# Feed-forward products of blocks 1 to 5 by seven half-size products instead of eight, with the attention chunks between them

## The chip, the cores and the metric

The kernel runs on one core of a Trainium2 chip. The metric is the device time of one execution in microseconds (us); of the kernel before, three executions took 854.86, 856.84 and 858.18 us, and their median, 856.84 us, is its time. The engines are named as the profile names them: PE (TensorE, matmuls) with PEld (its weight loads), DVE (VectorE), ACT (ScalarE), POOL (GpSimd) and SP (SyncE, which issues loads). Each engine works through its own instructions in a fixed order and waits for the others on semaphores.

## What is computed

A retention layer (attention with a decaying state) over 4 batches, 8 heads, 768 tokens and 64 channels a head, whose output, as 3072 tokens by 512 channels, goes through a feed-forward layer with a hidden width of 2048. q, k and v are float32; the two weight matrices come as float64.

```python
gamma = 1.0 - 2.0 ** (-5.0 - np.arange(H))
for t in range(S):
    state = gamma[None, :, None, None] * state + np.einsum('bhd,bhe->bhde', k[:, :, t], v[:, :, t])
    y[:, :, t] = scale * np.einsum('bhd,bhde->bhe', q[:, :, t], state)
x = np.ascontiguousarray(y.transpose(0, 2, 1, 3)).reshape(B * S, H * D)
h = x @ w_in                                   # 3072 x 512 by 512 x 2048
g = h * (1.0 / (1.0 + np.exp(-1.702 * h)))
return (g @ w_out).astype(np.float32)          # 3072 x 2048 by 2048 x 512
```

## The kernel before

The tokens are cut into 24 chunks of 128 (six in each batch), and four chunks make a block of 512 tokens, so there are six blocks, 0 to 5. A chunk goes through three stages. `turn` transposes q and k on PE (tile pt, L162) and brings them from PSUM to SBUF as qT and kT, and POOL makes kd, the k decayed to the chunk's end. `attend` multiplies kT and qT on PE (tile pa, L178), and DVE multiplies the result with a mask of decays (at, L181). `finish` adds the state's part and the chunk's own part on PE (tile py: the state's products at L191, those with at and v at L193), brings py into xT, and updates the state (products pu at L205, POOL and DVE behind them).

For a block, `up` makes the hidden units in 16 tiles of 128: four matmuls of 128x128 weights by 512 tokens into ph (L222), the sigmoid on ACT (sg, L224), the product on DVE (gT, L226). `down` makes the output of 128 tokens in 16 matmuls of 512 columns into po (L234), in four parts; a copy (o, L237) and a DMA follow. Each float32 matmul appears as two records in the profile. The main loop puts the stages of the chunks of block m between the units of block m-1, and a scheduler lays the final order on every engine. The loads of q, k and v of a chunk are three DMAs of 256 KB on SP.

The float64 weights are converted on chip (`narrow`, 32 pieces of 128x512): a piece is fetched into a raw buffer (L107), and six DVE steps (L119, L120, L123, L124, L127, L128), two ACT steps (L122, L125) and a POOL multiply (L126) make it float32. Pieces 0 to 15 are w_in's, 16 to 31 w_out's. The conversion runs along the chunks of block 0 and its feed-forward.

Of the kernel before, what the change touches and what calls it, by code (L numbers as in the profile page):

```python
# [9 lines left out]
F32 = mybir.dt.float32  # L10
# [3 lines left out]
P = 128  # L14
# [14 lines left out]
def kernel(  # L29
# [30 lines left out]
    BT = CB * P  # L60
    NB = NCH // CB
    NFF = DFF // P
    WAHEAD = 3
    assert 2 * D == P and HP * P == DM and S % P == 0 and NCH % CB == 0 and DM <= 512

    const = ctx.enter_context(tc.tile_pool(name="const", bufs=1))
    loads = ctx.enter_context(tc.tile_pool(name="loads", bufs=3))
    raw = ctx.enter_context(tc.tile_pool(name="raw", bufs=WAHEAD + 1))
    work = ctx.enter_context(tc.tile_pool(name="work", bufs=2))
    ps_a = ctx.enter_context(tc.tile_pool(name="ps_a", bufs=1, space=bass.MemoryType.PSUM))  # L70
    ps = ctx.enter_context(tc.tile_pool(name="ps", bufs=3, space=bass.MemoryType.PSUM))

# [1 line left out]
    QKV = {}  # L74

    def load(j):
        b, c = divmod(j, NC)
        for name, src in (("q", q), ("k", k), ("v", v)):
            t = loads.tile([P, H, D], F32, name=name + "_in")
            sp.dma_start(t, src[b, :, c * P:(c + 1) * P, :].rearrange("h p d -> p h d"))  # L80
            QKV[name, j] = t

    AHEAD = 2
    rowd = const.tile([P, HP, P], F32, name="rowd")
    cold = const.tile([P, 2 * H + HP], F32, name="cold")
    act.dma_start(cold, col_decay)
    for s in range(2):
        act.dma_start(
            rowd[s * D:(s + 1) * D],
            bass.AP(tensor=row_decay.tensor, offset=row_decay.offset + s * P,  # L90
                    ap=[[0, D], [2 * P, HP], [1, P]]),
        )

    # Weights by pieces of DM columns: w_in's by quarters of its columns, then w_out's by rows.
    W1 = const.tile([P, HP, DFF], F32, name="W1")
    W2 = const.tile([P, NFF, DM], F32, name="W2")
    w1v = moe_w_in.bitcast(U32).rearrange("(c p) (f two) -> p c f two", p=P, two=2)
    w2v = moe_w_out.bitcast(U32).rearrange("(f p) (e two) -> p f e two", p=P, two=2)
    PIECES = [(W1[:, c, f:f + DM], w1v[:, c, f:f + DM]) for f in range(0, DFF, DM) for c in range(HP)]
    N1 = len(PIECES)  # L100
    PIECES += [(W2[:, f, :], w2v[:, f]) for f in range(NFF)]
    RAW = {}

    def fetch(i):
        if i < len(PIECES):
            RAW[i] = raw.tile([P, DM, 2], U32, name="raw")
            sp.dma_start(RAW[i], PIECES[i][1])  # L107

    def narrow(i):
        """float64 to float32: the high word's 20 bits of fraction with the exponent rebiased, plus  # L110
        the low word at its place, added and so rounded in float32, then the sign."""
        fetch(i + WAHEAD)
        w, x = PIECES[i][0], RAW.pop(i)
        lo, hi = x[:, :, 0], x[:, :, 1]
        m = work.tile([P, DM], F32, name="m")
        e = work.tile([P, DM], F32, name="e")
        r = work.tile([P, DM], F32, name="r")
        mu = m.bitcast(U32)
# [4 lines left out]
        dve.tensor_scalar(mu, mu, 4, 1, op0=ALU.logical_shift_left, op1=ALU.logical_shift_right)  # L123
        dve.tensor_scalar(e.bitcast(U32), mu, 0x7F800000, None, op0=ALU.bitwise_and)  # L124
        act.activation(r, lo, AF.Copy, scale=2.0 ** -52)  # L125
        pool.tensor_mul(r, r, e)  # L126
        dve.tensor_add(m, m, r)  # L127
        dve.scalar_tensor_tensor(w.bitcast(U32), hi, 0x80000000, mu, op0=ALU.bitwise_and, op1=ALU.bitwise_or)  # L128

    load(0)  # L130
    for i in range(WAHEAD):
        fetch(i)
        if i < AHEAD - 1:
            load(i + 1)

# [1 line left out]
    ident = const.tile([P, P], F32, name="ident")  # L137
    make_identity(nc, ident)
    # mask[s, i, hp, t] = g^-(s+1) where s <= t, else 0, for head 2 hp + i
    mask = const.tile([P, 2, HP, P], F32, name="mask")  # L140
    for i in range(2):
        for hp in range(HP):
            h = 2 * hp + i
            dve.tensor_copy(mask[:, i, hp, :], cold[:, h:h + 1].to_broadcast([P, P]))
    m3 = mask.rearrange("s i h t -> s (i h) t")
    pool.affine_select(out=m3, in_=m3, compare_op=ALU.is_ge, fill=0.0, base=0,
                       pattern=[[0, H], [1, P]], channel_multiplier=-1)
    # two states in turn, block diagonal over a pair's heads
    state = [const.tile([P, HP, P], F32, name=f"state{i}") for i in range(2)]
    for t in state:  # L150
        dve.memset(t, 0.0)

# [1 line left out]
    QT, KT, KD, AT, XT = {}, {}, {}, {}, {}  # L154

    def turn(j):
        """q and k with channels on partitions, q decayed from the chunk's start; k decayed to its end."""
        qn, kn = QKV.pop(("q", j)), QKV.pop(("k", j))
        for x, store in ((qn, QT), (kn, KT)):
            p = ps.tile([P, HP, P], F32, name="pt", tag="att")  # L160
            for hp in range(HP):
                pe.transpose(p[:, hp, :], x[:, 2 * hp:2 * hp + 2, :].rearrange("p i d -> p (i d)"), ident)  # L162
            t = work.tile([P, HP, P], F32, name="qT" if store is QT else "kT")
# [154 lines left out]
```

## Time and profile before

| what | value |
|---|---|
| median of three runs | 856.84 us |
| lowest and highest run | 854.86 and 858.18 us |
| span of the profiled execution | 855.1 us |
| mean granted clock of TensorE in it | 0.976 |
| HBM read and written | 35.92 MB and 6.29 MB |

The profile shows one execution, from its first to its last instruction; the page gives its span, and no time of that execution beside it, so the span stands against the runs' median. In the page's list of engines each has its busy time, its share of the span and its count of records. The slices cut the span into 40 equal parts; a digit is the busy share in tenths. A group of instructions is given by line, engine, operation, output and inputs; behind the bar stand the busy time in us, the mean length of one in ns, and the idle time before them with what ended it. Lines of the timeline begin with the start and the length in us. Matmuls overlap one another, so the distance from start to start is what one costs in a stream.

### The profile page before, as it was taken

How to read it: one execution, taken by the hardware profiler on the slowest of the kernel's cores; microseconds unless marked ns; L12 is line 12 of the kernel's file. 1: busy time of each engine (PE TensorE's matmuls, PEld its weight loads, DVE VectorE, ACT ScalarE, POOL GpSimd, SP SyncE). 2: the span in 40 equal slices, each digit the busy share in tenths (PEclk: the TensorE clock that was granted, in tenths of full speed). 3: DMA queues.
4: the chain of work that ended last, by engine and by line, in shares of the span. 5: the costliest groups of instructions: out<-in, count | busy, mean ns of one | idle time of the engine just before them, and what ended most of it. 6: DMA issues, size and time to landing. Idle time of an engine off the chain costs nothing.

```text
span 855.1 us, 7038 instructions
## 1 busy us (share of the span) xinstructions
PE 821.2 (96%) x2816; PEld 408.3 (48%) x2816; DVE 239.1 (28%) x434; ACT 126.4 (15%) x210; POOL 84.6 (10%) x91
## 2 busy tenths in 40 slices
PE   4679979999999999999999999999999999999998
PEld 3545434445545544544545454445445445444443
DVE  4877888311222110222111222111122111012000
ACT  2234444000111000111000111100011100011000
POOL 3433333201101000101011000011010000000000
PEclk9759989999999999999999999999999999999999
DMA  9476454012010210110110110111100000000000
GB/s 224 133 183 162 149 164 144 25 38 61 13 25 13 50 38 25 50 25 13 38 49 25 37 36 14 25 46 41 38 13 0 1 12 25 12 1 0 13 13 25
DMA packets 83663, 42.66 MB, mean 50 GB/s; under 512 B 75952, under 2 KB 76464, under 8 KB 83632
## 3 DMA queue, kind: packets, MB, share of 16 engines
q1 hardware_dynamic: 79488, 35.66, 16.5%
q10 hardware_dynamic: 4144, 6.57, 2.1%
q8 instruction: 22, 0.36, 0.2%
q14 instruction: 9, 0.07, 0.0%
HBM read 35.92 MB, written 6.29 MB: 49 GB/s over the span
## 4 chain that ended last, share of the span: by engine, by line
PE 87%; DVE 7%; POOL 3%; issue 2%; DMA 1%; ACT 0%; SPq 0%; POOLq 0%; ACTq 0%; DVEq 0%
PE po L234 39%; PE ph L222 34%; PE py L193 4%; PE py L191 3%; PE pa L178 3%; POOL r L126 2%; PE pu L205 2%; PE pt L162 2%; DVE m L127 2%; DVE e L124 1%; DVE m L123 1%; DMA raw<-in_moe_w_in_dram 1%; DVE W L128 1%; DVE m L119 1%; DVE m L120 1%
## 5 line engine op out<-in xcount | busy, mean ns | idle before, releaser
L222 PE MATMUL ph<-xT,W 128*128 128x512 f32 x768 | 340.8, 601 | 0.0
L234 PE MATMUL po<-W,gT 128*128 128x512 f32 x768 | 336.0, 594 | 0.0
L222 PEld LDWEIGHTS ph<-xT,W 128*128 128x128 f32 x768 | 145.5, 193 | 174.0 <-issue 170.9
L234 PEld LDWEIGHTS po<-W,gT 128*128 128x128 f32 x768 | 143.5, 190 | 170.9 <-issue 169.7
L226 DVE TENSOR_TENSOR gT<-ph,sg 128x512 f32<-128x512 f32 x96 | 66.2, 690 | 209.5 <-ACT sg L224 209.5
L224 ACT ACTIVATE sg<-ph 128x512 f32<-128x512 f32 x96 | 57.2, 595 | 261.8 <-PE ph L222 261.7
L237 DVE COPY o<-po 128x512 f32<-128x512 f32 x24 | 16.6, 692 | 239.2 <-PE po L234 239.2
L171 POOL TENSOR_TENSOR kd<-k_in,cold 128x512 f32<-128x512 f32 x20 | 21.1, 1054 | 451.8 <-PE pu L205 258.1
L193 PE MATMUL py<-at,v_in 128*64 128x128 f32 x384 | 46.8, 321 | 14.4 <-DVE at L181 14.4
L181 DVE TENSOR_TENSOR at<-pa,mask 128x512 f32<-128x512 f32 x48 | 31.2, 683 | 67.1 <-PE pa L178 67.1
L126 POOL TENSOR_TENSOR r<-r,e 128x512 f32<-128x512 f32 x32 | 42.3, 1322 | 72.6 <-DVE e L124 72.4
L198 ACT ACTIVATE xT<-py 128x512 f32<-128x512 f32 x24 | 14.3, 596 | 189.3 <-PE py L193 189.3
L191 PE MATMUL py<-qT,state 128*128 128x128 f32 x160 | 41.3, 344 | 0.0
L178 PE MATMUL pa<-qT,kT 64*128 64x128 f32 x384 | 30.4, 302 | 8.6 <-DVE qT L165 7.8
L191 PEld LDWEIGHTS py<-qT,state 128*128 128x128 f32 x160 | 28.0, 209 | 20.5 <-issue 19.7
L178 PEld LDWEIGHTS pa<-qT,kT 64*128 64x128 f32 x384 | 25.6, 203 | 24.9 <-issue 14.6
L193 PEld LDWEIGHTS py<-at,v_in 128*64 128x64 f32 x384 | 22.5, 148 | 29.6 <-DVE at L181 17.4
L167 ACT ACTIVATE kT<-pt 128x512 f32<-128x512 f32 x24 | 14.3, 596 | 142.4 <-PE pt L162 142.4
L127 DVE TENSOR_TENSOR m<-m,r 128x512 f32<-128x512 f32 x32 | 26.2, 819 | 19.4 <-POOL r L126 19.4
L125 ACT ACTIVATE r<-raw 128x512 f32<-128x512 uint32 x32 | 21.8, 681 | 53.9 <-DVE m L127 43.8
L205 PE MATMUL pu<-v_in,kd 128*128 128x128 f32 x160 | 25.8, 307 | 0.0
L212 POOL TENSOR_TENSOR state<-state,cold 64x256 f32<-64x256 f32 x32 | 20.1, 629 | 49.9 <-DVE state L214 31.8
(25 smaller groups left out, 218.0 us busy)
## 6 DMA issues: line engine op xcount, KB each, us to landing
raw<-in_moe_w_in_dram SPq DMA_DIRECT2D x16, 512.0 KB, 4.5
raw<-in_moe_w_out_dram SPq DMA_DIRECT2D x16, 512.0 KB, 3.3
q_in<-in_q_dram SPq DMA_DIRECT2D x24, 256.0 KB, 4.0
k_in<-in_k_dram SPq DMA_DIRECT2D x24, 256.0 KB, 4.4
v_in<-in_v_dram SPq DMA_DIRECT2D x24, 256.0 KB, 3.3
out_dram<-o ACTq DMA_DIRECT2D x24, 256.0 KB, 2.0
rowd<-in_row_decay_dram ACTq DMA_DIRECT2D x2, 128.0 KB, 5.5
cold<-in_col_decay_dram ACTq DMA_DIRECT2D x1, 10.0 KB, 2.8
```

Of the source, the lines that this page charges most:

```text
L125: act.activation(r, lo, AF.Copy, scale=2.0 ** -52)
L126: pool.tensor_mul(r, r, e)
L127: dve.tensor_add(m, m, r)
L178: pe.matmul(p[:, i, hp, :], KT[j][r, hp, :], QT[j][r, hp, :], start=True, stop=True)
L181: dve.tensor_mul(AT[j][:, i], p[:, i], mask[:, i])
L191: pe.matmul(y[:, hp, :], old[:, hp, :], qt[:, hp, :], start=True, stop=False)
L193: pe.matmul(y[i * D:(i + 1) * D, hp, :], vn[:, 2 * hp + i, :], a[:, i, hp, :], start=not c, stop=True)
L205: pe.matmul(u[:, hp, :], kd[:, h, :].rearrange("p i d -> p (i d)"), vn[:, h, :].rearrange("p i d -> p (i d)"), start=True, stop=True)
L222: pe.matmul(p, W1[:, c, f * P:(f + 1) * P], XT[m][:, c, :], start=(c == 0), stop=(c == HP - 1))
L224: act.activation(s, p, AF.Sigmoid, scale=1.702)
L226: dve.tensor_mul(g, p, s)
L234: pe.matmul(p, GT[m, f][:, n * P:(n + 1) * P], W2[:, f, :], start=(f == 0), stop=(f == NFF - 1))
```

## The change

Block 0 keeps plain products (`up0`, `down0`). For blocks 1 to 5 each of the two feed-forward products is cut in two along tokens, along the summed dimension and along the outputs, and the 2x2 product of parts is made by seven products of parts instead of eight, in Winograd's form of Strassen's method. Slots 0 to 3 of W1, W2, X and G hold the four parts, slots 4 to 6 sums of them (slot 3 is overwritten by a sum as well). `sums_w1` and `sums_w2` make those of the weights once, `sums_x` those of a block's x, all on POOL; `sums_g` changes the hidden units in place on DVE and POOL. The products have 256 columns instead of 512. In `up` four pairs of tiles each go through seven products of four matmuls; ACT copies the accumulator x out between them (p1, u, vv), PE then goes on adding in it, and DVE adds the other accumulators (px and py in the rows; py is also the name of a chunk's output). In `down` the seven products run as 28 units, and a stage of a chunk of the next block follows every second unit.

PE's order is now the order of the code (`manual_schedule`); the scheduler still sets the others. Chunks from 8 on are transposed by DVE in blocks of 32x32, from q and k loaded in 32 DMAs of 16 KB a chunk (q_sq, k_sq), with k loaded once more as it is where kd needs it. For other chunks the transposes stay on PE, and ACT evicts both. The decay of q moves from qT to the eviction of py into X. Within py the four state products come first, then the eight others. In the conversion DVE has four steps, ACT two and POOL two (a clamp, L172, and the multiply, L177); pieces hold other columns, are staged in the slots of W2 that the sums fill later, and have three raw buffers and two sets of temporaries.

```diff
+    ctx.enter_context(tc.manual_schedule(engines={mybir.EngineType.PE}))
...
+        if j < 2 * CB:
+            plain("q", q, "q_sq", 2)
+            plain("kn", k, "k_sq", 2)
+        else:
+            for name, src in (("q", q), ("k", k)):
+                t = two.tile([P, HP, P // C4, C4], F32, name=name + "_sq")
+                for r0 in range(0, P, C4):
+                    d0 = r0 % D
+                    for hp in range(HP):
+                        sp.dma_start(t[r0:r0 + C4, hp],
+                                     src[b, 2 * hp + r0 // D, rows, d0:d0 + C4].rearrange("(s p) d -> p s d", p=C4))
...
-        dve.tensor_scalar(mu, hi, 0x7FFFFFFF, None, op0=ALU.bitwise_and)
-        dve.tensor_scalar(m, m, F64_MOST, F64_LEAST, op0=ALU.min, op1=ALU.max)
-        act.activation(m, m, AF.Copy, scale=2.0 ** 16)
-        dve.tensor_scalar(mu, mu, 4, 1, op0=ALU.logical_shift_left, op1=ALU.logical_shift_right)
-        dve.tensor_scalar(e.bitcast(U32), mu, 0x7F800000, None, op0=ALU.bitwise_and)
+            act.activation(m, hi.bitcast(F32), AF.Abs, scale=2.0 ** 16)
+            pool.tensor_scalar(m, m, F64_MOST * 2.0 ** 16, F64_LEAST * 2.0 ** 16, op0=ALU.min, op1=ALU.max)
+            dve.tensor_scalar(mu, mu, 3, None, op0=ALU.logical_shift_left)
+            dve.scalar_tensor_tensor(mu, hi, 0x80000000, mu, op0=ALU.bitwise_and, op1=ALU.bitwise_or)
+            dve.tensor_scalar(eu, mu, 0xFF800000, None, op0=ALU.bitwise_and)
...
+                dve.transpose(t.rearrange("p h t -> p (h t)"), QKV.pop((name, j)).rearrange("p h s d -> p (h s d)"))
...
+    def sums_b(b):
+        pool.tensor_sub(b[4], b[3], b[0])
+        pool.tensor_sub(b[6], b[2], b[3])
+        pool.tensor_sub(b[5], b[2], b[4])
+        pool.tensor_sub(b[3], b[1], b[5])
...
+    def up(d):
+        def product(acc, sa, sb, start, stop):
+            for u in range(2):
+                for c in range(2):
+                    pe.matmul(acc[:, u, :], W1[:, 2 * d + u, sa, c, :], X[:, sb, c, :],
+                              start=(start and u == 0 and c == 0), stop=(stop and c == 1), skip_group_check=True)
+        g = [G[:, 2 * d:2 * d + 2, s, :] for s in range(4)]
+        x = ps.tile([P, 2, TH], F32, name="px", tag="x")
+        product(x, 0, 0, True, False)
+        p1 = one.tile([P, 2, TH], F32, name="p1", tag="s1")
+        act.activation(p1, x, AF.Copy)
+        y = ps.tile([P, 2, TH], F32, name="py1", tag="y")
+        product(y, 1, 1, True, True)
+        dve.tensor_add(g[0], y, p1)
+        hidden(g[0], g[0])
+        product(x, 5, 5, False, False)
...
+        product(x, 2, 2, False, True)
+        hidden(g[1], x)
...
+            for p in range(2 * d, 2 * d + 2):
+                for n in range(2):
+                    pe.matmul(p0[:, n, :], G[:, p, sa, n * P:(n + 1) * P], W2[:, sb, p, :],
+                              start=(new and p == 0 and n == 0), stop=(last and p == NP - 1), skip_group_check=True)
...
+    for j in range(CB):
+        if j + 2 <= CB:
+            load(j + 2)
+        turn(j)
+        attend(j)
+        narrow(1)
+        finish(j)
+        narrow(1)
+    for f in range(NFF):
+        up0(f)
+        narrow(1)
...
+    for m in range(1, NB):
+        for d in range(NP // 2):
+            up(d)
...
+        for n, unit in enumerate(down(m)):
+            unit()
+            if between and n % 2:
+                between.pop(0)()
+                if not between:
+                    sums_x()
```

How this stands on the engines is seen in three places. In the rows, x8 counts matmuls (each is two records in the profile), and the sizes are those of the operand or of the result.

First PE in the middle of the program: before, from block 0's products down (po) with chunks 5 and 6's transposes, products and state between them.

```order
L234 MATMUL po<-W_79,gT 128x512 x16
L162 MATMUL pt<-ident,q_in 128x128 x4
L162 MATMUL pt<-ident,k_in 128x128 x4
L234 MATMUL po<-W_79,gT 128x512 x8
L178 MATMUL pa<-qT,kT 128x128 x8
L234 MATMUL po<-W_79,gT 128x512 x8
L191 MATMUL py<-qT,state_114 128x128
L193 MATMUL py<-at,v_in 64x128 x2
```

And after, block 1 at the seam between its products up (px, py with a number) and down (pd), with chunk 8.

```order
L312 MATMUL px<-X,W_72 128x256 x4
L312 MATMUL py_1337<-X,W_72 128x256 x4
L312 MATMUL px<-X,W_72 128x256 x4
L363 MATMUL pd<-W_73,G 128x256 x16
L210 MATMUL pa<-qT,kT 128x128 x8
L363 MATMUL pd<-W_73,G 128x256 x8
L223 MATMUL py<-qT,state_80 128x128 x4
L227 MATMUL py<-at,v_in 64x128 x8
L237 MATMUL pu<-v_in,kd 128x128 x4
L363 MATMUL pd<-W_73,G 128x256 x16
```

The products have become half as wide, the transposes are gone from PE, and the state's products stand together ahead of the others.

Second DVE, where the conversion of the weights ends. Before, its steps lie between the products with the sigmoid (gT) and those with the mask (at) of the chunks that run beside it; these are rows around the 14th piece.

```order
L181 TENSOR_TENSOR at<-pa,mask 128x512
L127 TENSOR_TENSOR m<-m,r 128x512
L120 TENSOR_SCALAR m<-m 128x512
L128 SCALAR_TENSOR_TENSOR W_78<-raw,m 128x512
L226 TENSOR_TENSOR gT<-ph,sg 128x512
L123 TENSOR_SCALAR m<-m 128x512
L119 TENSOR_SCALAR m<-raw 128x512
L124 TENSOR_SCALAR e<-m 128x512
L120 TENSOR_SCALAR m<-m 128x512
L226 TENSOR_TENSOR gT<-ph,sg 128x512
```

After, these are the rows up to the last of block 0's 16 products with the sigmoid (G); the two L180 ahead of it finish the 27th and 28th piece.

```order
L253 TENSOR_TENSOR G<-ph,sg 128x2x256
L180 TENSOR_TENSOR W_73<-W_73 128x2x256
L175 TENSOR_SCALAR W_73<-W_73 128x512
L180 TENSOR_TENSOR W_73<-W_73 128x2x256
L173 TENSOR_SCALAR W_73<-W_73 128x512
L253 TENSOR_TENSOR G<-ph,sg 128x2x256
```

The four steps of a piece (L173, L174, L175, L180) now stand ahead of the products with the sigmoid: the first of the 16 comes behind eight pieces, the last behind 28, and chunk 4's products with the mask behind all 32.

Third SP, from the last weights on. Before, a chunk is three loads.

```order
L107 DMA raw<-in_moe_w_out_dram 128x1024 x4
L80 DMA q_in<-in_q_dram 128x8x64
L80 DMA k_in<-in_k_dram 128x8x64
L80 DMA v_in<-in_v_dram 128x8x64
L80 DMA q_in<-in_q_dram 128x8x64
```

After, these are the last loads in the old form (chunks 6 and 7) and then chunk 8 and part of chunk 9.

```order
L153 DMA W_73<-in_moe_w_out_dram 128x1024 x16
L109 DMA q_in<-in_q_dram 128x8x64
L109 DMA kn_in<-in_k_dram 128x8x64
L109 DMA v_in<-in_v_dram 128x8x64
L109 DMA q_in<-in_q_dram 128x8x64
L109 DMA kn_in<-in_k_dram 128x8x64
L109 DMA v_in<-in_v_dram 128x8x64
L120 DMA q_sq<-in_q_dram 32x4x32 x16
L120 DMA k_sq<-in_k_dram 32x4x32 x16
L109 DMA v_in<-in_v_dram 128x8x64
L120 DMA q_sq<-in_q_dram 32x4x32 x16
```

A chunk's q and k have become 32 small DMAs that stand in SP's queue ahead of the same chunk's v.

More of the change, by code (lines that the diff above doesn't have):

```diff
@@ L77, in load @@
         b, c = divmod(j, NC)
[L78 to L92, printed above, removed]
@@ L130 @@
[L130 to L147, printed above, removed]
@@ L149 @@
[L149 to L154, printed above, removed]
-    def turn(j):
[L158 to L163, printed above, removed]
-            if store is QT:
-                dve.tensor_mul(t, p, rowd)
+    stage = W2[:, 4:7].rearrange("p s n e -> p (s n e)")
@@ L173, in attend @@
+        if CB <= j < NCH and (j % CB < 2 or j < 2 * CB - 1):
+            load(j + (2 if j >= 2 * CB else 1))
     def attend(j):
@@ L178, in attend @@
                 pe.matmul(p[:, i, hp, :], KT[j][r, hp, :], QT[j][r, hp, :], start=True, stop=True)
-        AT[j] = work.tile([P, 2, HP, P], F32, name="at")
+        AT[j] = one.tile([P, 2, HP, P], F32, name="at")
         for i in range(2):
@@ new lines @@
+    act.dma_start(cold, col_decay)
+    for s in range(2):
+        act.dma_start(
+            rowd[s * D:(s + 1) * D],
+            bass.AP(tensor=row_decay.tensor, offset=row_decay.offset + s * P,
+                    ap=[[0, D], [2 * P, HP], [1, P]]),
+        )
+    load(0)
+    fetch()
+    load(1)
+    fetch()
+    fetch()
+    make_identity(nc, ident)
+    for i in range(2):
+        for hp in range(HP):
+            h = 2 * hp + i
+            dve.tensor_copy(mask[:, i, hp, :], cold[:, h:h + 1].to_broadcast([P, P]))
@@ new lines, with chunks @@
+    m3 = mask.rearrange("s i h t -> s (i h) t")
+    pool.affine_select(out=m3, in_=m3, compare_op=ALU.is_ge, fill=0.0, base=0,
+                       pattern=[[0, H], [1, P]], channel_multiplier=-1)
+    for t in state:
+        dve.memset(t, 0.0)
+    for j in range(CB):
[9 more added lines that the diff above has]
+        narrow(1)
+    narrow(1)
+    def chunks(m):
+        return [s for j in range(m * CB, (m + 1) * CB)
+                for s in (lambda j=j: turn(j), lambda j=j: attend(j), lambda j=j: finish(j))]
@@ new lines @@
+    between = chunks(1)
+    for f in range(NFF):
+        down0(f)
+        narrow(1)
+        if between and f >= 2:
+            between.pop(0)()
+        if f % 4 == 3:
+            sums_w1(f // 2 - 1)
+    sums_x()
+    for m in range(1, NB):
+        for d in range(NP // 2):
+            up(d)
+            if m == 1:
+                sums_w2(2 * d)
+            if m + 1 < NB and d < 2:
+                load((m + 1) * CB + d)
+        between = chunks(m + 1) if m + 1 < NB else []
+        for n, unit in enumerate(down(m)):
+            unit()
+            if between and n % 2:
+                between.pop(0)()
+                if not between:
+                    sums_x()
```

259 lines of the change are left out of this document (174 added, 85 removed).

## The prediction

> **What bounds the kernel now.** I read the page first: engine totals, the 40 slices, the chain that ended last, the costliest groups.
>
> ```profile
> span 855.1 us, 7038 instructions
> ...
> PE 821.2 (96%) x2816; PEld 408.3 (48%) x2816; DVE 239.1 (28%) x434; ACT 126.4 (15%) x210; POOL 84.6 (10%) x91
> ...
> PE   4679979999999999999999999999999999999998
> ...
> PEclk9759989999999999999999999999999999999999
> ...
> PE 87%; DVE 7%; POOL 3%; issue 2%; DMA 1%; ACT 0%; SPq 0%; POOLq 0%; ACTq 0%; DVEq 0%
> ...
> L222 PE MATMUL ph<-xT,W 128*128 128x512 f32 x768 | 340.8, 601 | 0.0
> L234 PE MATMUL po<-W,gT 128*128 128x512 f32 x768 | 336.0, 594 | 0.0
> ```
>
> TensorE (PE) is busy in 96% of the span and carries 87% of the chain. Only the first seven slices, some 150 us, are thin, at a reduced clock. Then the two stages by windows (span of the window, then busy us of PE, PEld, DVE, ACT and POOL, the clock, the DMA share, GB/s):
>
> ```profile
> 120.00:140.00 20.00, 17.13 (x49) 7.98 (x48) 17.14 (x35) 8.56 (x15) 7.38 (x6) 0.83 0.47 149
> ...
> 200.00:300.00 100.00, 100.00 (x359) 49.80 (x358) 20.53 (x33) 13.13 (x22) 5.47 (x7) 1.00 0.12 29
> ```
>
> Up to about 140 us VectorE (DVE, 17.1 of 20 us) and the weight conversion limit; later PE is full and DVE has four fifths of its time free. So work taken from PE in blocks 1 to 5 is worth its whole length, if the added evictions and sums fit on the others; work in block 0 is worth what the conversion lets through.
>
> A matmul's busy time overlaps the next one's, so I take prices from starts in the timeline of PE (start, length, what, count). A float32 matmul is two records, and counts below are records.
>
> ```profile
> 143.53 0.60 PE L162 MATMUL pt<-ident,q_in 128*128 128x128 f32 x4
> ...
> 144.40 7.03 PE L234 MATMUL po<-W,gT 128*128 128x512 f32 x16
> 151.37 1.16 PE L178 MATMUL pa<-qT,kT 64*128 64x128 f32 x16
> 152.46 7.13 PE L234 MATMUL po<-W,gT 128*128 128x512 f32 x16
> 159.52 1.09 PE L193 MATMUL py<-at,v_in 128*64 128x128 f32 x16
> 160.54 1.16 PE L205 MATMUL pu<-v_in,kd 128*128 128x128 f32 x8
> 161.54 13.90 PE L234 MATMUL po<-W,gT 128*128 128x512 f32 x32
> 175.28 0.60 PE L162 MATMUL pt<-ident,q_in 128*128 128x128 f32 x4
> ...
> 191.17 0.39 PE L191 MATMUL py<-qT,state 128*128 128x128 f32 x2
> ...
> 194.22 1.16 PE L205 MATMUL pu<-v_in,kd 128*128 128x128 f32 x8
> ```
>
> A 512-column record: (175.28 - 161.54) / 32 = 0.4294 us. A chunk: transposes 0.87, pa 1.09, py without state 1.02, pu 1.00 (0.125 a record), py with its state products between 194.22 - 191.17 = 3.05.
>
> **The change, stage by stage.** *Products.* Each block has 2 x 256 / 2 = 256 records of 512 columns, 109.9 us; afterwards 2 stages x 7 products x 16 matmuls x 2 = 448 records of 256. A 256-column record doesn't occur before. From below it is half of 0.4294, 0.2147; from above a 128-column record of pu, in which the weight load is least hidden, and another 128 columns at the 512 rate: 0.125 + 0.107 = 0.232. What could stick out is the weight load:
>
> ```profile
> 512.23 0.19 PEld L222 LDWEIGHTS ph<-xT,W 128*128 128x128 f32 x1 [0.24 <-issue]
> ```
>
> It takes 0.19 us and lies inside the 0.4294, and in the pu stretch loads as long come every 0.125 us. It fits inside 0.215, so I take 0.2155: 2240 x 0.2155 = 482.7 us for five blocks (upper end 519.7) against 549.6.
>
> *Attention.* Chunks 8 to 23 lose their PE transposes (16 x 0.87 = 13.9 us); the 32x32 transposes go to DVE, with no row of their own: between DVE's one-input 0.42 (a row below) and POOL's two-input 1.32 us each, eight a block, beside PE. The state products now stand together, so I price their eight records as pu's, 1.00, and py is 2.02 instead of 3.05 (upper end 3.05, +17 us for the 17 such chunks from chunk 4 on). Chunks 4 to 7 cost 4 x (0.87 + 1.09 + 1.02) + 3 x 1.00 + 3 x 1.00 = 17.9; chunks 8 to 23 16 x 2.11 + 14 + 13 = 60.8.
>
> *Start.* Block 0's four chunks are now a strict sequence on PE, cold, and chunk 0's products with the mask stand behind the first conversion on DVE.
>
> ```profile
> 7.52 1.11 PE L162 MATMUL pt<-ident,k_in 128*128 128x128 f32 x4 [2.19 <-DMA k_in<-in_k_dram]
> 11.57 2.08 PE L178 MATMUL pa<-qT,kT 64*128 64x128 f32 x16 [2.94 <-DVE qT L165]
> ...
> 15.12 1.23 PE L205 MATMUL pu<-v_in,kd 128*128 128x128 f32 x4
> 16.28 1.97 PE L193 MATMUL py<-at,v_in 128*64 128x128 f32 x14
> ...
> 30.18 0.80 PE L191 MATMUL py<-qT,state 128*128 128x128 f32 x2
> ...
> 65.15 8.00 PE L222 MATMUL ph<-xT,W 128*128 128x512 f32 x16
> ```
>
> ```profile
> 2.82 7.09 DMA raw<-in_moe_w_in_dram
> ```
>
> The first weights land at 9.9, the conversion takes some 5.5 (its seven steps at the durations below), the mask products 1.4 (2 x 0.69), py and pu cold 2.2 + 2.4: chunk 0 ends near 21. Each later one: transposes 2.2, eviction 0.75 (0.6 and a hop), pa 2.1, state 2.9 (8 records at some 0.73 the two from start to start; it hides the mask products), py 2.2, pu 2.4 = 12.6. So block 0's first product starts near 21 + 38 = **59** (before 65.15). Faster if the clock rises (52), slower if the loads are late, since a v load waits on SP for the finish of the chunk two before and the next weights queue behind it (66).
>
> *Block 0 and the conversion.* Its 128 records of products up take 55.0, plus 1 cold (16 took 8.0 at 65.15): PE is done at 115. But DVE runs in a fixed order in which the 16th product with the sigmoid stands behind 28 of the 32 conversions, and down0's third and fourth accumulators take the buffers of the 15th and 16th. So the pace of conversion decides.
>
> ```profile
> 104.61 0.69 DVE L127 TENSOR_TENSOR m<-m,r 128x512 f32<-128x512 f32 x1 [0.85 <-POOL r L126]
> 105.22 0.42 DVE L123 TENSOR_SCALAR m<-m 128x512 uint32<-128x512 uint32 x1
> 105.55 0.69 DVE L128 SCALAR_TENSOR_TENSOR W<-raw,m 128x512 uint32<-128x512 uint32 x1
> ```
>
> ```profile
> 63.58 1.25 POOL L126 TENSOR_TENSOR r<-r,e 128x512 f32<-128x512 f32 x1
> ...
> 138.67 1.32 POOL L126 TENSOR_TENSOR r<-r,e 128x512 f32<-128x512 f32 x1 [2.14 <-DVE e L124]
> ```
>
> Between these two rows lie 18 conversions: 4.17 us each before. DVE now has four of its six steps, at 0.61 and 0.33 us from start to start: 1.9 us, and 0.46 for its share of the sigmoid products. POOL has more: the multiply, the clamp (new there), and half a weight sum a piece.
>
> ```profile
> L171 POOL TENSOR_TENSOR kd<-k_in,cold 128x512 f32<-128x512 f32 x20 | 21.1, 1054 | 451.8 <-PE pu L205 258.1
> ...
> L126 POOL TENSOR_TENSOR r<-r,e 128x512 f32<-128x512 f32 x32 | 42.3, 1322 | 72.6 <-DVE e L124 72.4
> ```
>
> The clamp has one input and no row; between half of kd (0.53) and the contended multiply (1.32); I take 0.65, nearer the first. POOL: 1.32 + 0.65 + 0.66 = 2.6 us a piece, and two sets of temporaries with a chain of 5 us give 2.5. Before, the pace was 1.17 times the load of its busiest engine (17.1 of 20 us x 4.17 = 3.6); 2.6 x 1.17 = 3.05, and with one more change of engine I take **3.2** (2.6 to 4.17). The eighth conversion is through 4.5 us after the start of block 0's products, at 63.5; 20 more end at 127.5, the product with the sigmoid at 128.1, where PE stood at 116.7: a **wait of 11.4 us** on PE (0 to 31).
>
> The Trainium skill, "GPSIMD Engine Reference", section "4.1 Engine selection", has GpSimd roughly at line rate with one input and about half as fast as VectorE with two. By that rule the clamp would be an estimated half of the two-input rows, 0.53 to 0.66, and the sum would be the same; for two inputs the trace agrees (1.05 to 1.32 against DVE's 0.69), for one no row here shows it.
>
> *Evictions in blocks 1 to 5.* One group of seven products takes 28 x 2 x 0.2155 = 12.1 us of PE.
>
> ```profile
> L226 DVE TENSOR_TENSOR gT<-ph,sg 128x512 f32<-128x512 f32 x96 | 66.2, 690 | 209.5 <-ACT sg L224 209.5
> L224 ACT ACTIVATE sg<-ph 128x512 f32<-128x512 f32 x96 | 57.2, 595 | 261.8 <-PE ph L222 261.7
> ```
>
> ACT has seven such operations (4.2 us), DVE eight (5.5): covered. The new wait: PE goes on in accumulator x only when ACT has copied it out. One product of 1.72 us stands between; drain, hop and copy need about 0.9, so 0.8 is spare. If that cover went, behind the waiting matmul the whole PE queue would stand, at three places in each of 20 groups. I allow 0.6 (one late eviction) at each of ten ends of stages: 6 us, from 0 to 20.
>
> *Loads.* A chunk from 8 on has up to 34 DMAs on SP instead of 3.
>
> ```profile
> 1.92 0.86 SPq L80 DMA_DIRECT2D v_in<-in_v_dram  x1
> ...
> 310.61 0.37 SPq L80 DMA_DIRECT2D q_in<-in_q_dram  x1
> ...
> q_in<-in_q_dram SPq DMA_DIRECT2D x24, 256.0 KB, 4.0
> ```
>
> At 0.37 + 0.05 each that is 14 us; the program has eight completion counters, so that a DMA waits for the eighth before it, and at 4.0 us to landing that allows one in 0.5, 17 us a chunk, 68 a block that lasts about 111. I take nothing, with the rival below.
>
> *End and sum.*
>
> ```profile
> 851.28 0.69 DVE L237 COPY o<-po 128x512 f32<-128x512 f32 x1 [13.04 <-PE po L234]
> ```
>
> From PE's last result (about 851.1) to the end 4.0 us, as now. Span: 59 + 56 + 11.4 + (55.0 + 17.9) + (482.7 + 60.8) + 6 + 4.0 = 752.8 against 855.1. The median of the runs, 856.84, is 1.7 above the profiled span; so **754.5 us**.
>
> **Rivals.** (1) *The conversion no longer binds*: POOL's 2.6 a piece without bubbles puts the 16th product at 116; no wait, and with it most of the allowance gone: about 737. For it: shorter DVE work; against: the fixed order and POOL's share of weight sums.
> (2) *The conversion stays at 4.17*, because POOL's clamp is as slow as its multiply and the raw buffers are three: 20 x 0.97 = 19 more, 774.
> (3) *The small loads become the bound*: DVE's transposes stand in order ahead of the next mask products. At 0.9 us each, the third load's issue at the start, 34 make 30 us a chunk, 122 a block against 111: some 11 a block, 45 in four: 800. Against: 0.37 when nothing presses.
> (4) *The other side: weight loads surface.* Half-width products load as many weights for half the columns. If the load of 0.19 stood ahead of each 256-column record, that would be 0.405, 2240 x 0.19 = 424 us more: 1178. It decides from 0.262 a record on, where 2240 x 0.046 eats the 102 gained. Against: the rows of 512 and of pu. The Trainium skill, "TensorE: Matmul & The Clock Gate", section "The mechanism", has weight loads overlap with matmuls under way only where the row groups differ, and here all are full; by that rule the 512-column record would be about 0.62 (0.43 and the load's 0.19). This trace has 0.4294 with a load in each, so it does not agree at that width, and the rival keeps a small chance.
>
> **How the numbers follow.** Forecast, 743 to 766: 0.50. Rival 1: 0.17; rival 2: 0.18; rival 3 and other waits in the blocks: 0.11; rival 4: 0.04. Range 734 to 792: it takes in rivals 1 and 2, the 0.232 record (+37) and the two ends of the start. Half a per cent, 4 us, is about what a measurement of this kernel can tell from no change: faster by more 0.95, within 0.01, slower 0.04.
>
> **What would show it.** Right: px and pd records 0.215 us apart; PE full from down0 on; one idle stretch of about 11 us on PE at po, released by DVE's G; the first ph near 59; last conversion near 140; SP's small DMAs done ahead of each transpose. Wrong: px or pd records over 0.23 apart, idle time ahead of px that ACT ends, DVE transposes that wait for DMA, conversions over 4 us apart.

## The result, and the profile after

Four runs of the changed kernel took 781.95 to 782.79 us, median 782.11; four of the kernel before 854.86 to 858.18, median 856.47. The ratio is **0.9127** (95% interval 0.9112 to 0.9142): 74 us faster, where 102 had been predicted. The profiled execution of the changed kernel has a span of 780.3 us. First its page:

```profile
span 780.3 us, 9581 instructions
...
PE 725.1 (93%) x3648; PEld 572.4 (73%) x3648; DVE 368.6 (47%) x547; ACT 153.4 (20%) x253; POOL 206.3 (26%) x195
...
PE   4679677499999999999999999999999999999998
...
PEclk9879878699999999999999999999999999999999
...
PE 77%; DVE 11%; POOL 7%; issue 3%; DMA 1%; SPq 0%; ACT 0%; POOLq 0%; DVEq 0%
...
L260 PE MATMUL ph<-X,W 128*128 128x512 f32 x128 | 65.8, 671 | 16.9 <-DVE G L253 16.9
L272 PE MATMUL po<-W,G 128*128 128x512 f32 x128 | 61.8, 628 | 10.4 <-DVE G L253 10.4
```

From the ninth slice on PE is full at full clock, as it was before. Ahead of it PE is thinner than before. DVE and POOL together hold 18% of the chain that ended last (10% before). Block 0's products, ph and po, wait 27.3 us for DVE's products with the sigmoid, and a record of ph has a mean of 671 ns against 601 for those of ph before.

The stages by windows of the same profile (span, then busy us of PE, PEld, DVE, ACT and POOL, granted clock, DMA share, GB/s), and PE's timeline at their borders:

```profile
55.00:152.00 97.00, 70.41 (x139) 28.19 (x138) 74.88 (x103) 33.43 (x58) 62.36 (x58) 0.85 0.36 122
152.00:228.00 76.00, 74.66 (x332) 40.48 (x333) 27.67 (x38) 7.79 (x14) 38.00 (x33) 0.96 0.23 49
228.00:780.00 552.00, 548.11 (x2968) 477.82 (x2966) 234.64 (x351) 94.57 (x155) 75.43 (x69) 1.00 0.18 38
```

```profile
55.56 14.76 PE L260 MATMUL ph<-X,W 128*128 128x512 f32 x34
...
147.77 2.07 PE L272 MATMUL po<-W,G 128*128 128x512 f32 x2 [5.23 <-DVE G L253]
152.65 10.48 PE L272 MATMUL po<-W,G 128*128 128x512 f32 x18 [2.81 <-DVE G L253]
...
227.68 1.89 PE L312 MATMUL px<-X,W 128*128 128x256 f32 x8
229.41 1.89 PE L312 MATMUL py<-X,W 128*128 128x256 f32 x8
```

The first ph starts at 55.56, the first px of block 1 at 227.68. That gives the prediction's sum term by term:

| stage | predicted, us | measured, us |
|---|---|---|
| start of block 0's products | 59 | 55.6 |
| from there to the first px (56 + 11.4 + 72.9) | 140.3 | 172.1 |
| blocks 1 to 5 and the end (482.7 + 60.8 + 6 + 4.0) | 553.5 | 552.6 |
| span | 752.8 | 780.3 |

So the miss lies in block 0, between 56 and 228 us: 31.8 us too many there, of which the early start gives 3.4 back. Eight 256-column records take (229.41 - 227.68) / 8 = 0.216 us each, as taken (0.2155). That the last stage comes within 0.9 is partly luck. Summed from start to start, its products take 487.8 us instead of 482.7, since those down cost 0.220 a record; and the allowance of 6 us for late evictions, almost unused, covers that.

DVE at the 8th and at the 28th conversion (L180 ends one, L253 is the product with the sigmoid):

```profile
61.99 0.68 DVE L180 TENSOR_TENSOR W<-W 128x512 f32<-128x512 f32 x1
62.70 0.69 DVE L253 TENSOR_TENSOR G<-ph,sg 128x512 f32<-128x512 f32 x1
...
150.57 1.09 DVE L180 TENSOR_TENSOR W<-W 128x512 f32<-128x512 f32 x1 [1.45 <-POOL W L177]
...
151.92 0.68 DVE L253 TENSOR_TENSOR G<-ph,sg 128x512 f32<-128x512 f32 x1
```

The 8th is where it was put (63.5 predicted, through at 62.7). But the next 20 take (150.57 - 61.99) / 20 = **4.43 us** each instead of 3.2, more than the 4.17 before, and the 16th product with the sigmoid comes at 151.9 instead of 128.1. DVE's and POOL's groups in that stretch, 62 to 151 us (count, busy us, mean ns, idle before):

```profile
L174 DVE SCALAR_TENSOR_TENSOR W<-W 128x512 uint32<-128x512 uint32 x20 | 20.7, 1036 | 0.4
L180 DVE TENSOR_TENSOR W<-W 128x512 f32<-128x512 f32 x21 | 19.1, 910 | 15.1 <-POOL W L177 15.1
L173 DVE TENSOR_SCALAR W<-W 128x512 uint32<-128x512 uint32 x19 | 13.2, 695 | 4.5 <-POOL W L172 4.5
L175 DVE TENSOR_SCALAR W<-W 128x512 uint32<-128x512 uint32 x20 | 12.1, 603 | 0.3
L253 DVE TENSOR_TENSOR G<-ph,sg 128x512 f32<-128x512 f32 x15 | 10.2, 681 | 0.2 <-ACT sg L252 0.2
...
L177 POOL TENSOR_TENSOR W<-W 128x512 f32<-128x512 f32 x20 | 27.0, 1351 | 17.0 <-DVE W L175 17.0
```

The steps of the conversion have become longer than the same kinds of operation were before (0.69 and 0.42), while the product with the sigmoid between them keeps 0.681. What differs is where an operand lies: L253 reads ph from PSUM, the others read SBUF alone. The timeline shows a stretched step beside an operation of POOL each time; the first two rows are from block 0, the rest from the stretch around chunk 9 with the sums of block 1's hidden units (rows of DVE and POOL that overlap in time are set together):

```profile
103.30 1.26 POOL L284 TENSOR_TENSOR W<-W 128x512 f32<-128x512 f32 x1
...
103.36 1.48 DVE L173 TENSOR_SCALAR W<-W 128x512 uint32<-128x512 uint32 x1 [1.74 <-POOL W L172]
...
298.13 0.68 DVE L301 TENSOR_TENSOR G<-G 128x512 f32<-128x512 f32 x1
...
298.36 1.58 POOL L304 TENSOR_TENSOR G<-G 128x512 f32<-128x512 f32 x1 [5.13 <-DVE G L303]
...
298.85 1.64 DVE L302 TENSOR_TENSOR G<-G 128x512 f32<-128x512 f32 x1
...
301.29 1.27 POOL L304 TENSOR_TENSOR G<-G 128x512 f32<-128x512 f32 x1 [1.35 <-DVE G L303]
...
301.13 1.28 DVE L213 TENSOR_TENSOR at<-pa,mask 128x512 f32<-128x512 f32 x2
```

POOL's sum runs from 103.30 to 104.56, and DVE's shift, begun 0.06 later, ends at 104.84: its own 0.3 after POOL's end. At 298 POOL starts while a sum of DVE is under way and takes 1.58, and DVE's next sum, begun in the middle of POOL's, takes 1.64. At 301 DVE's two products read pa from PSUM, and both engines keep their usual lengths (0.64 and 1.27).

This gave a first theory, **turns**: an operation of DVE that has all its operands in SBUF and an operation of POOL do not run at the same time; the one that starts second waits, and the wait counts as its own length. Its rivals were **side by side** (the engines are independent, and something else is slow), **two sets** (the two sets of temporaries hold the chain of a piece up) and, for the long rows, **chain** (they are waits for the other engine's results).

### The profile page after: what moved, and what is told of

Same layout as the page of the kernel before. It is cut to its first block, busy times and chain, and to the rows that moved or that the text cites. A ratio compares the mean times of both kernels' runs of the same rounds, so it can differ in the third digit from the quotient of the medians.

```text
span 780.3 us, 9581 instructions
## 1 busy us (share of the span) xinstructions
PE 725.1 (93%) x3648; PEld 572.4 (73%) x3648; DVE 368.6 (47%) x547; ACT 153.4 (20%) x253; POOL 206.3 (26%) x195
## 4 chain that ended last, share of the span: by engine, by line
PE 77%; DVE 11%; POOL 7%; issue 3%; DMA 1%; SPq 0%; ACT 0%; POOLq 0%; DVEq 0%
PE pd L363 30%; PE px L312 18%; PE py L312 13%; PE po L272 5%; PE py L227 4%; POOL W L177 3%; PE pu L237 3%; PE pa L210 3%; DVE W L174 3%; DVE W L180 2%; DVE W L173 2%; PE py L223 2%; DVE W L175 1%; POOL W L172 1%; DMA W<-in_moe_w_in_dram 1%
## 5 line engine op out<-in xcount | busy, mean ns | idle before, releaser
L363 PE MATMUL pd<-W,G 128*128 128x256 f32 x1120 | 250.3, 381 | 0.4 <-DVE G L303 0.3
L363 PEld LDWEIGHTS pd<-W,G 128*128 128x128 f32 x1120 | 210.1, 190 | 30.8 <-DVE G L303 1.2
L312 PE MATMUL px<-X,W 128*128 128x256 f32 x640 | 148.7, 379 | 0.0
L312 PEld LDWEIGHTS px<-X,W 128*128 128x128 f32 x640 | 121.6, 190 | 17.0 <-issue 0.5
L312 PE MATMUL py<-X,W 128*128 128x256 f32 x480 | 113.4, 379 | 0.0
L312 PEld LDWEIGHTS py<-X,W 128*128 128x128 f32 x480 | 91.2, 190 | 12.4
L260 PE MATMUL ph<-X,W 128*128 128x512 f32 x128 | 65.8, 671 | 16.9 <-DVE G L253 16.9
L272 PE MATMUL po<-W,G 128*128 128x512 f32 x128 | 61.8, 628 | 10.4 <-DVE G L253 10.4
L177 POOL TENSOR_TENSOR W<-W 128x512 f32<-128x512 f32 x32 | 43.5, 1360 | 25.8 <-DVE W L175 25.8
L253 DVE TENSOR_TENSOR G<-G,sg 128x512 f32<-128x512 f32 x60 | 41.3, 689 | 17.4 <-ACT sg L252 17.4
L180 DVE TENSOR_TENSOR W<-W 128x512 f32<-128x512 f32 x32 | 30.3, 946 | 26.4 <-POOL W L177 26.1
```

Source lines behind the costliest of these rows:

```text
L180: dve.tensor_add(w, m.rearrange(shape, **sizes), r.rearrange(shape, **sizes))
L253: dve.tensor_mul(g, h, s)
L260: pe.matmul(h, w, X[:, c // 2:4:2, c % 2, :], start=(c == 0), stop=(c == 3))
L272: pe.matmul(PO[n], G[:, p, 2 * half + ab, t0:t0 + P], w, start=(f == 0), stop=(f == NFF - 1))
L312: pe.matmul(acc[:, u, :], W1[:, 2 * d + u, sa, c, :], X[:, sb, c, :], start=(start and u == 0 and c == 0), stop=(stop and c == 1), skip_gr ...
L363: pe.matmul(p0[:, n, :], G[:, p, sa, n * P:(n + 1) * P], W2[:, sb, p, :], start=(new and p == 0 and n == 0), stop=(last and p == NP - 1), ...
```

## Experiments

All are edits of the changed kernel. The runs of the kernel before beside them have medians of 857.05 to 857.21 us. A time without a range beside it is that of one execution.

### A third set of temporaries

```diff
-    NRAW, NTMP = 3, 2
+    NRAW, NTMP = 3, 3
...
-            for i in range(NTMP)]
+            for i in range(2)]
+    TMPS.append([X[:, 4 + t].rearrange("p c t -> p (c t)") for t in range(3)])
```

> A third set of temporaries for the conversion (in X's slots 4 to 6, which are filled only later). 'Turns': the work is the same, 4.2 to 4.5 us a piece, span within 5 of 780. 'Two sets': two thirds of the pace, 3.0 a piece, span about 753.

Measured: 784.26 us. A piece took 4.13 us between the 8th conversion (61.83) and the 28th (144.35), but the scheduler now put the 16th product with the sigmoid behind 30 conversions, and it came at 154.92, 3.0 later than in the changed kernel. The gain of 29 us that two sets demanded isn't there; the third set shortened a piece by 0.3, and the order gave that back.

### Multiply and clamp on DVE

```diff
-            pool.tensor_scalar(m, m, F64_MOST * 2.0 ** 16, F64_LEAST * 2.0 ** 16, op0=ALU.min, op1=ALU.max)
+            dve.tensor_scalar(m, m, F64_MOST * 2.0 ** 16, F64_LEAST * 2.0 ** 16, op0=ALU.min, op1=ALU.max)
...
-            pool.tensor_mul(r, r, e)
+            dve.tensor_mul(r, r, e)
```

> The conversion's multiply and clamp move from POOL (1.36 and 0.69 us) to DVE (two inputs 0.61, one input 0.34 from start to start). 'Turns': 1.1 us less a piece and fewer waits for the other's end, and the 16th product with the sigmoid now stands behind 23 conversions instead of 28: it comes near 122 instead of 152, span about 752. 'Two sets': the chain loses two changes of engine, 3.0 a piece, no wait on PE, span about 742. The prediction's view: DVE becomes the busiest with 3.3 a piece, span about 745. If POOL was not in the way at all, DVE only gets longer: span 780 or more.

Measured: **748.22 us** (747.44 to 749.0), ratio 0.8732 (0.8713 to 0.8751): 34 us less than the changed kernel, from putting more work on the engine that was already the busier of the two. PE's waits in block 0 (total, times, longest):

```profile
PE po L272 <- DVE G L253: 6.3, 3, 2.7
PE py L227 <- DVE at L213: 1.2, 2, 1.0
PE ph L260 <- DVE G L253: 0.9, 1, 0.9
```

27.3 us of waits for G have become 7.2. The 16th product with the sigmoid is at 117.15 instead of 151.92. Part of this is order: it now stands behind 23 conversions instead of 28. What is left of stretched rows on DVE stands beside POOL's sums of w_in's parts, of which 12 still run there. The run refutes that POOL was not in the way at all (780 or more), but its span of 747.1 lies between the 752 of turns and the 745 of the prediction's view and doesn't choose between these two.

### 16 more multiplies on POOL

```diff
     for f in range(NFF):
         up0(f)
         narrow(1)
+        i = narrowed[0] - 1
+        spare = X[:, 6].rearrange("p c (ab f) -> p c ab f", ab=2) if i < N1 else X[:, 6]
+        pool.tensor_mul(spare, PIECES[i][0], PIECES[i][0])
```

> One more POOL multiply of 128x512 after each of 16 conversions, whose result nobody reads: 16 x 1.35 = 21.6 us of POOL, which was busy 12.6 of 20 us there. 'Turns': all of it is added, the 28th conversion near 172, span about 800. 'Two sets': only what delays the chain on POOL, 0 to 8 us. Side by side: POOL has the room, 0 to 5 us.

Measured: 798.65 us, span 796.9, 16.6 more. The 28th conversion moved from 150.57 to 163.93, by 13.4 us; nobody reads the result of the extra multiplies. POOL was busy 64% of that stretch (62.4 of 97 us), so independent engines would have had room for most of the 16 x 1.27 = 20.3 us; two thirds of it were paid. That is more than side by side (at most 5) and two sets (at most 8) allowed, and less than the whole that turns had put there (28th near 172).

### The sums of w_in's parts after the last product with the sigmoid

```diff
         if f % 4 == 3:
-            sums_w1(f // 2 - 1)
+            p = f // 2 - 1
+            pool.tensor_copy(W1[:, p:p + 2, 4, 0, 0:1], G[:, NP - 2:NP, 3, TH - 1:TH])
+            sums_w1(p)
```

> The sums of w_in's parts stay on POOL, but each group of four now begins with a tiny copy that reads the last hidden units of block 0, so that they run behind the 16th product with the sigmoid instead of between the conversions. With the change as it was: 28th conversion at 150.6 us, span 780.3. 'Turns': 12 x 1.4 = 17 us come out from between the conversions: 28th near 134, 3.6 a piece, span about 764. 'Two sets': 4.2 a piece, span about 776. Side by side: POOL was not the bound, span within 3 of 780.

Measured: 780.26 us (span 778.5), where turns had a span of 764: a miss by 14, and a time within what side by side had. A piece took (139.86 - 60.00) / 20 = 3.99 us and not 3.6, and the 16th product came 10.7 us earlier (141.21); but the time hardly moved. PE's waits between 53 and 226 us:

```profile
PE po L272 <- DVE G L253: 11.3, 4, 4.3
PE ph L260 <- DVE G L253: 10.5, 6, 2.7
PE py L227 <- DVE at L213: 6.5, 1, 6.5
```

The waits for G fell from 27.3 to 21.8, and a new one of 6.5 stands at py: the sums now meet the last four conversions, and chunk 4's products with the mask stand in order on DVE behind all 32. The pace, between the 3.6 of turns and the 4.2 of two sets, decides for neither. The same edit together with multiply and clamp on DVE:

> Both edits: the conversion's multiply and clamp on DVE, and the sums of w_in's parts late. 'Turns': POOL is nearly silent while weights are converted, so DVE's steps run unstretched: 16th product with the sigmoid near 108 instead of 118 (multiply and clamp alone), PE waits for none of them, span about 738 against 747. If DVE's own work is the bound by now: span within 3 of 747.

Measured: 752.28 us (751.07 to 752.97, span 750.7), ratio 0.8779 (0.8755 to 0.8803), a miss: slower than with the sums where they were (748.22). The 16th product is at 109.25, near where turns had put it and 7.9 earlier than there, but PE then waits 6.4 us at pa and 3.8 at py. Moving POOL's work later only moves the place at which DVE pays for it.

### Both engines side by side, measured alone

In the last 25 us of the program, where DVE and POOL have almost nothing to do, both start at the same moment on tiles of their own:

```diff
+        for i in range(14):
+            pool.tensor_add(a[4 + i % 2], a[0], a[1])
+        for i in range(4):
+            dve.tensor_add(b[4 + i % 2], b[0], b[1])
+        for i in range(4):
+            dve.tensor_add(b[4 + i % 2], y, b[0])
...
+        for i in range(4):
+            dve.transpose(sq[4 + i % 2], sq[0])
+        for i in range(4):
+            dve.tensor_scalar(b[4 + i % 2].bitcast(U32), b[0].bitcast(U32), 3, None, op0=ALU.logical_shift_left)
```

> The changed kernel with a measurement in its last 25 us, where DVE and POOL have next to nothing to do: POOL adds 14 times two SBUF tiles of 128x512 into a third, one behind the other, and from the same moment DVE does four sums of two SBUF tiles, four of a PSUM and an SBUF tile, four STREAM_TRANSPOSE and four one-input TENSOR_SCALAR from SBUF, all on tiles of its own, with no dependence between the engines. "Turns" (an SBUF-only operation of DVE and one of POOL don't run at the same time): the four SBUF sums take about 4 x 1.6 = 6 to 7 us from first start to last end, where four alone take 2.5, and so do the TENSOR_SCALAR that still meet POOL (1.4 and more each, alone 0.41); the four with PSUM stay at 0.69 and the transposes at 0.70; POOL's sums that meet DVE's SBUF sums take 1.5 to 1.9, the others 1.27. "Chain" (the stretched rows in the conversion are waits for the other engine's results, which the profile counts into the operation): with no dependence between them every row keeps its length, DVE's 0.69, 0.69, 0.70, 0.41 and POOL's 1.27. The time of the whole says nothing, since the scheduler sets block 0 in a slightly different order too.

The timeline of this kernel from 755 us on (a row with x4 is four operations in a run, with their common length):

```profile
755.36 5.72 DVE L408 TENSOR_TENSOR W<-W 128x512 f32<-128x512 f32 x4
755.46 19.90 POOL L406 TENSOR_TENSOR W<-W 128x512 f32<-128x512 f32 x14
761.00 2.47 DVE L410 TENSOR_TENSOR W<-py,W 128x512 f32<-128x512 f32 x4
763.39 0.41 DVE L415 TENSOR_SCALAR W<-W 128x512 uint32<-128x512 uint32 x1
...
763.84 1.38 DVE L415 TENSOR_SCALAR W<-W 128x512 uint32<-128x512 uint32 x1
765.14 2.48 DVE L413 STREAM_TRANSPOSE X<-X 128x512 f32<-128x512 f32 x4
767.55 1.79 DVE L415 TENSOR_SCALAR W<-W 128x512 uint32<-128x512 uint32 x2
```

Nothing here waits for the other engine's results, and yet four sums from SBUF take 5.72 us, while four that read one operand from PSUM take 2.47 and four transposes 2.48, all beside the same stream on POOL. That refutes chain. The one-input TENSOR_SCALAR meet it too: two took 1.38, and the two that kept their length (0.41 and 0.38) started within 0.02 us of a sum of POOL's, which took 1.54 and 1.52 in their place. POOL's sums beside DVE's four sums took 1.71 to 1.72 each instead of 1.27. So turns holds for every kind tried except one: the transposes read and write SBUF alone and yet keep their length.

### The sums of w_in's parts on DVE too

Multiply, clamp and these 16 sums on DVE:

```diff
-        pool.tensor_add(w[4], w[3], w[2])
-        pool.tensor_sub(w[6], w[0], w[3])
-        pool.tensor_sub(w[5], w[4], w[0])
-        pool.tensor_sub(w[3], w[1], w[5])
+        dve.tensor_add(w[4], w[3], w[2])
+        dve.tensor_sub(w[6], w[0], w[3])
+        dve.tensor_sub(w[5], w[4], w[0])
+        dve.tensor_sub(w[3], w[1], w[5])
```

> The kernel with clamp and multiply on DVE, and the 16 sums of w_in's parts on DVE as well (they stand behind the last product with the sigmoid there, instead of beside the conversions on POOL). "Turns": a sum costs the pair of engines 0.6 us on DVE instead of 1.3 to 1.7 on POOL, and none of it falls ahead of block 0's last G, so the 16th G comes some 10 us earlier than the 117 it has with the sums on POOL; PE's waits for G (7.2 us there) go, and what is left is the wait for chunks 4 and 5's masks behind the sums on DVE: 741 us (736 to 748). "Side by side" (POOL's sums cost DVE nothing): DVE gets 10 us more work ahead of chunk 5's masks and the time becomes 748 to 756.

Measured: **744.0 us** (742.64 to 744.13), ratio 0.8677 (0.8657 to 0.8698), the fastest of all kernels here. Its window over block 0's products up, and one piece in DVE's timeline:

```profile
50.00:105.00 55.00, 55.00 (x128) 24.50 (x128) 54.28 (x110) 27.92 (x46) 2.47 (x3) 0.98 0.47 153
```

```profile
89.77 0.68 DVE L180 TENSOR_TENSOR W<-W 128x512 f32<-128x512 f32 x1
90.37 0.68 DVE L174 SCALAR_TENSOR_TENSOR W<-W 128x512 uint32<-128x512 uint32 x1
90.97 0.68 DVE L253 TENSOR_TENSOR G<-ph,sg 128x512 f32<-128x512 f32 x1
91.57 0.41 DVE L175 TENSOR_SCALAR W<-W 128x512 uint32<-128x512 uint32 x1
91.91 0.42 DVE L172 TENSOR_SCALAR W<-W 128x512 f32<-128x512 f32 x1
92.24 0.68 DVE L177 TENSOR_TENSOR W<-W 128x512 f32<-128x512 f32 x1
92.84 0.42 DVE L173 TENSOR_SCALAR W<-W 128x512 uint32<-128x512 uint32 x1
93.18 0.68 DVE L180 TENSOR_TENSOR W<-W 128x512 f32<-128x512 f32 x1
```

With POOL silent (2.5 of 55 us) every row of DVE has its own length, one follows the other without a gap, and a piece takes 93.18 - 89.77 = 3.41 us: seven operations on one engine are faster than five on it and two on the other. PE runs the 55 us of block 0's products up without a wait. What is left of waits there is 6.7 us at chunk 6's transposes, which wait for chunk 5's X (L230); in DVE's order that stands behind seven of the sums, which now meet POOL's sums of w_out's parts and take 1.63 to 1.75 each. Just before, it is POOL that is shut out: two of its sums, from 135.41 on, take 7.45 us together, while nine operations of DVE in SBUF that follow one another without a gap keep their own lengths. Moving those sums too wasn't tried.

### The attention terms

Two runs took back one part of the change each. The chunks from 8 on transposed on PE from plain loads:

```diff
-        if j < 2 * CB:
+        if True:
...
-            if j < 2 * CB:
+            if True:
```

> Chunks 8 to 23 are transposed on PE again, with q and k as one plain load each (no small DMAs, no DVE transposes, no second load of k). Terms of the prediction: 16 x 0.87 = 13.9 us back on PE and nothing saved elsewhere: span 794. If the small loads or the DVE transposes delayed PE somewhere: less, 780 to 788.

Measured: 796.52 us. The first px is where it was (227.6), and blocks 1 to 5 are 14.6 us longer, 0.91 a chunk (0.87 in the prediction): the 32 small loads and the transposes on DVE cost PE nothing. And the state's products back between the others:

```diff
-        if c:
-            for hp in range(HP):
+        for hp in range(HP):
+            if c:
                 pe.matmul(y[:, hp, :], old[:, hp, :], qt[:, hp, :], start=(hp == 0), stop=False,
                           skip_group_check=True)
-        for hp in range(HP):
             for i in range(2):
```

> Within py the state's products go back between the others, one pair of heads after the other. Term of the prediction: 17 chunks x 1.03 = 17.5 us back from chunk 4 on, and 0 to 6 more in block 0: span 798 to 803. If the order of these products costs nothing and the 3.05 us had another cause: span 780.

Measured: 814.17 us (span 812.2), 9 above the upper end of the expected span. In blocks 1 to 5 it is as expected, 567.7 us against 552.6, 1.08 for each of the 14 chunks there that have state products. The rest is in block 0: its first ph starts at 64.4 instead of 55.6, and the way from there to px is 8.0 longer, 7.4 of it in longer waits for DVE. PE's rows for the fourth chunk, of this kernel and of the changed one:

```profile
53.83 0.49 PE L223 MATMUL py<-qT,state 128*128 128x128 f32 x2
57.23 1.28 PE L226 MATMUL py<-at,v_in 128*64 128x128 f32 x4 [2.90 <-DVE at L213]
58.44 0.80 PE L223 MATMUL py<-qT,state 128*128 128x128 f32 x2
```

```profile
47.55 1.16 PE L223 MATMUL py<-qT,state 128*128 128x128 f32 x8
51.44 0.43 PE L227 MATMUL py<-at,v_in 128*64 128x128 f32 x2 [2.73 <-DVE at L213]
```

Standing together, the state's products run while DVE makes the mask products; standing between, three of four come after that wait. In the cold start this was worth 8.8 us and not only the 1.03 a chunk.

## Why the prediction was off where it was

The forecast of 754.5 us was 27.6 short (3.5%); the time is in the range, in the case that keeps the old pace of conversion (774) and 8 beyond it. That the range took it in is luck as far as the mechanism goes: it was widened for records of 0.232 us and for a slow clamp, and neither came.

**The step that failed** is in the part on block 0 and the conversion: "POOL: 1.32 + 0.65 + 0.66 = 2.6 us a piece" beside DVE's "1.9 us, and 0.46", of which the larger, times 1.17, gave 3.05, and one more change of engine 3.2. It took DVE and POOL as two engines that work side by side. For the conversion's operations, all in SBUF, they take turns, and then their times add: DVE's four steps 1.88, POOL's multiply and clamp 1.28 and 0.62 (medians in the changed kernel), and 12 sums of 1.28 among those 20 pieces, 0.77, are together 4.55; measured were 4.43. With all on DVE, four rows of 0.61 and three of 0.33 from start to start give 3.43; measured were 3.41. The addition is an estimate, good to a tenth here: with the sums late it gives 3.78 against 3.99 measured, with 16 more multiplies 5.57 against 5.10. The rows of before already held the warning: L127, in SBUF, had a mean of 0.82 in its conversion, L226, with PSUM, 0.69, and POOL's multiply 1.32 against 1.05 for kd. The prediction called the multiply "contended" and went on as if that cost DVE nothing.

The Trainium skill has this rule, in "SBUF — State Buffer", section "Who interferes with whom": DVE and GpSimd share one pair of ports to SBUF as a lock held for a whole instruction, and a DVE instruction with two SBUF inputs, or one in a two-port mode, contends for it, while one with at most one SBUF input outside those modes does not. The runs agree for the sums, 5.72 against 2.47 us for four, and for the transposes with their one input, 2.48; that the one-input TENSOR_SCALAR contend (0.41 to 1.5 us) fits the rule if they run in such a mode, which no run here shows.

**What followed from it.** By the prediction's own terms this stage has 128.9 us without its wait. The waits came to 28.0 (16.9, 10.4 and 0.7) instead of 11.4, spread over eight ph and three po rather than one idle stretch, because a late product with the sigmoid also keeps the accumulators of ph. Of the remaining 15.2, 3.4 are also there in the kernel with everything on DVE, whose PE, hardly waiting, needs 139.0 - 6.7 = 132.3 us for the same stage. The other 11.8 go with the clock: 0.85 from 55 to 152 us here, against 0.98 from 50 to 105 there. The prediction had a cold end of 1 us. That waiting lowers the clock was not tested by itself; the two went together in these runs.

**What was right.** The 256-column record (0.216 up and 0.220 down; 0.2155), with weight loads hidden: PEld is busy 73% of the span, and PE waits for none, so the rival with surfacing loads falls. The state's products (1.08 a chunk; 1.03) and the transposes (0.91; 0.87). That small loads don't bind: those of the sixteen chunks landed after 1.7 and 1.8 us in the median, and PE never waits for them. The end (3.8 us after PE's last record; 4.0). **Off in size:** the allowance of 6 us for late evictions, of which PE shows 0.3 (pd, for G at L303); and the start, 59 against 55.6: chunk 0 ends at 19.8 instead of 21, and a later chunk takes 11.9 instead of 12.6, since pa takes 1.1 rather than 2.1 and pu 1.7 rather than 2.4, while the state's products with the wait for the mask behind them, 3.9, are longer than the 2.9 taken.

Of the rivals, the one in which the conversion stays at its old pace came nearest, for a wrong reason: the clamp was not slow (0.62, near the 0.65 taken), and no engine waited for a raw piece to land between 55 and 152 us.

## What to carry to other kernels

Where VectorE and GpSimd both work on SBUF tiles, add their times instead of taking the larger (here that came within a tenth of the measured pace); work that GpSimd does at half of VectorE's speed is then cheaper on VectorE even if that is the busier engine, and what may stay beside GpSimd are operations that read PSUM, and transposes. A row that is longer than the same operation elsewhere in the trace is to be read against what the other engine does in that moment before its mean is used as a price. And of work moved out of a critical stretch, look up what it meets where it lands: twice here the gain came back as a wait at the next chunk.

## What the runs showed of the hardware

- Of the changed kernel's DVE operations in SBUF, transposes apart, each one that starts behind one of POOL ends after it: 0.69 becomes up to 1.75 us, a one-input TENSOR_SCALAR of 0.41 up to 1.50. When POOL starts second, its 1.27 becomes up to 1.72 beside single sums of DVE, and two sums took 7.45 beside a row of DVE operations without a gap.
- With one operand in PSUM (0.62 each in a run) and for STREAM_TRANSPOSE (0.62) nothing changes beside POOL.
- POOL's clamp, with one input, takes 0.62 us for 128x512, its sum or multiply of two tiles 1.27.
- A weight load of 0.19 us in front of every matmul record of 0.216 to 0.220 us stays hidden through 2240 records.
